# A state-space scan feeding a bilinear FFN on one core: constants made in another order on GpSimd, decay exponents kept in the PSUM banks of C·B, and a new instruction plan

## The chip, the core and the metric

The kernel runs on one core of a Trainium2 chip. A core has five engines that run their own instruction queues in order and wait for each other through semaphores: TensorE (PE, with its weight loads shown apart as PEld), VectorE (DVE), ScalarE (ACT), GpSimd (POOL) and SyncE (SP, which here issues the DMAs). Matmuls write into PSUM, eight banks of 512 fp32 columns by 128 partitions. The metric is the device time of one execution in microseconds.

## The reference, cut to what matters

Two stages follow each other. The first is a chunked scan over a sequence of 768 steps, for 4 batches and 8 heads, with a head size of 32 and a state of 16:

```python
for c in range(nc):
    cum = np.cumsum(la, axis=-1)                      # la = log(clip(a, 1e-6, 1)) of this chunk
    L = np.exp(cum[:, :, :, None] - cum[:, :, None, :]) * causal
    M = np.einsum('bhin,bhjn->bhij', Cc, Bc) * L
    y[:, :, sl] = M @ xc + (Cc @ state) * np.exp(cum)[..., None]
    state = np.exp(sum(la)) * state + sum_j decay_from_j * Bc (x) xc
```

The second is a feed-forward net over the 3072 tokens, with the scan's 256 features as input:

```python
h = (x @ w1) * (x @ w2) @ w3       # 256 -> 1024, 1024 -> 1024
out = h @ w_out                    # 1024 -> 256
```

The weights arrive as float64. The kernel multiplies w3 and w_out once on the chip, so that the net is one "up" step (two products and their product by elements) and one "down" step.

## The kernel before

**Tiling.** The sequence is cut into 16 chunks of 48 steps; two chunks make a slice of 96 steps, which with 4 batches gives 384 tokens. There are 8 slices. Per slice the net has 8 up steps `l<slice>.<ft>` (two halves `.0` and `.1` of six matmuls of 384 columns each) and 3 down steps `z<slice>.<tk>`. Numbers are kept as a sum of two reduced-precision parts, a high and a low one, which is why each product needs three matmuls.

**The order.** Everything is a named task, and the string `PLAN` lists the tasks; each engine executes its share of them in that order. Suffixes `:v`, `:a` and `:p` put a task on VectorE, ScalarE or GpSimd, and `+n` puts n matmuls on zeros there, which only keep TensorE occupied. The banks of the up and down steps come from a ring over banks 4, 5 and 6 (lines 189 to 197).

**A chunk `c<k>`.** `D0`, `D1` (line 392): TensorE forms the exponents (differences of cumulated logs) of 8 of the 16 head pairs each; for the first two chunks as an fp32 product with a triangular constant `LS` and a bf16 product with an identity `IM`, from chunk 2 on as one bf16 product of `LD` and `RD`. `E0`, `E1` (line 404): ScalarE takes their exponential into `rr`. `C` (line 422): 16 small products give C·B. `M0` to `M3` (line 411): VectorE multiplies C·B by the exponentials. `B0`, `B1` (line 407): GpSimd forms the decayed B. `Y` (line 435): 32 pairs of products give the output and the next state in one bank, called py. `Z` (VectorE) and `x0` to `x3` carry the state to the next chunk; `h` (ScalarE) and `l` (VectorE) write the high and low parts of the output, the input of the up steps. The function `at_of` (line 223) deals the banks 0 to 3 out in turn to the seven outputs of a chunk.

**Weights.** Each of 32 pieces of weights goes through six steps: `D` (DMA), `A` (scale, VectorE or ScalarE), `Y` (a copy of half words), `L` and `S` (bit operations, VectorE), `H` (high part) and `P` (low part). Names are `w0` to `w7` for w1 and w2 (`w0` and `w1` as two halves a and b), `o0` to `o3` for w_out and `v0` to `v15` for w3, whose products with w_out (`v<j>.M`) TensorE adds up in bank 7.

**The start.** `k.u` makes a triangular mask `UT`, `k.q` the constant `LS`, `k.p` makes `LD`, `k.c` makes `IM`, `k.r` a mask for the scan and `k.g` makes `RD`, all on GpSimd with memsets and selects (lines 271 to 317). `b.clip`, `b.ln` and `b.m<chunk><half>` prepare the first two chunks' logs, and `a.clip`, `a.ln`, `a.scan`, `a.t0`, `a.r0`, `a.t1`, `a.r1`, `a.save` the cumulated logs of all others, which go to memory and come back as rows of `LD` and `RD` (`c<k>.K`).

**The end.** `store_b` (line 638) writes a down step's 128 tokens; those of the last step lie in two batches, so there are two DMAs, of 32 and of 96 rows, both issued by SyncE.

Of the kernel before, what the change touches and what calls it, by code (L numbers as in the profile page):

```python
# [29 lines left out]
k.z b.D k.u b.tab k.p a.D w0b.D s0.N0 k.c w0a.D b.clip k.r c0.T b.ln b.m00:v w1a.D a.clip:p c0.X b.m01:v k.q  # L30
a.ln a.exp a.scan +8 c0.D1 c1.T k.X b.m10:v c1.X w0b.A:v w0b.Y:v s0.N1 +1 c0.D0 c0.E1 w0b.L a.t0:v k.L1:a c0.B1
b.m11:v c0.E0 w2.D a.r0:v c0.C w0a.A:v c0.B0 w0b.S c1.D1 k.g a.t1:v w0a.Y:v c0.S c0.M3 c0.M2 w0a.L a.r1:v c1.D0
c0.M0 c0.x0:a a.save w1a.A:v w1b.D c0.M1 c1.E1 w0a.S w3.D c1.C c1.E0 w0b.H:v w1a.Y:a c1.B1 c0.Y c1.B0 c1.M3
c0.x1:a c1.M2 k.R0:p c1.M1 w0a.H:a c1.M0 c2.X c0.h w1a.L k.R1:p +1 c1.Y c0.l s1.N w0b.P:v c2.K w0a.P:v c1.h
w1a.S c1.l +2 l0.0.1 w1b.A:a w2.A:v w1b.Y:a l0.0.0 w1a.H:v w1a.P:v w2.Y:a l0.0.0q w1b.L l0.0.1q w1b.S c2.T c1.Z
l0.1.0 l0.0.a w4.D c1.x2:p w2.L c1.x1:a c1.x3:a c1.x0:p w2.S w1b.H:a w5.D l0.1.a w1b.P:v w3.A:a +2 l0.1.1 l0.0.g
w2.H:v w3.Y:a c3.T c2.D1 w2.P:v c3.K c2.D0 l0.2.0 l0.1.g c2.E0 c2.E1 w3.L c2.B0 l0.2.1 w3.S c2.B1 l0.2.a w6.D
w3.H:v w4.A:a c2.C w3.P:v w4.Y:a l0.3.0 c2.M2 c2.M3 c2.M0 c2.M1 l0.3.1 c3.X w5.A:a w4.L w4.S l0.3.a c2.Y w5.Y:a
l0.2.g w4.H:p l0.3.g s2.N c2.Z w4.P:v c2.x0:p c2.h w7.D c3.D1 c3.D0 c2.x1:p c2.x2:a l0.4.1 c2.l c3.E0 o0.D w5.L
c3.E1 c4.K c3.B0 w6.A:a l0.4.0 w5.S c3.B1 c2.x3:a c4.T w5.H:v w6.Y:a c3.C w5.P:v c4.X l0.5.0 c3.M0 l0.4.a c3.M3  # L40
w6.L l0.5.1 w6.S l0.5.a c3.M2 o1.D w7.A:a w6.H:p c3.M1 l0.5.g c3.Y w7.Y:a w6.P:v l0.4.g l0.6.1 v0.D c3.Z o0.A:a
w7.L c3.x2:p l0.6.0 c3.h c5.K w7.S o0.Y:a c3.l w7.H:p l1.0.0 v1.D c3.x3:v l0.6.a c5.T w7.P:v c3.x0:a o3.D c4.D0
c3.x1:a c4.D1 o0.L l1.0.1 c4.E0 o0.S l1.0.a c4.B0 c4.E1 c5.X l1.1.1 l0.6.g o0.H:p o1.A:a l1.0.g c4.B1 o1.Y:a
o0.P:v c4.C l1.1.0 c4.M2 c4.M1 c4.M0 v0.A:v l0.7.0 v2.D l1.1.a o1.L v0.Y:a o2.D c4.M3 l0.7.1 l1.1.g o1.S v1.A:a
c4.Y v0.L o1.H:p v3.D v1.Y:a v0.S l1.2.0 o1.P:v v0.H:a v6.D v1.L l0.7.a c5.D1 l1.2.a c5.D0 v0.P:v l1.2.1 c5.E0
c4.Z c5.E1 c5.B0 v1.S c4.h l1.3.1 c4.x0:p o3.A:a c4.x1:p l1.2.g v7.D v1.H:p o3.Y:a v0.M c4.l c5.B1 l0.7.g
c4.x3:p v1.P:v v2.A:a o3.L l1.3.0 v2.Y:a o3.S c4.x2:v v1.M v5.D l1.3.a v2.L o2.A:a l1.3.g o3.H:a o2.Y:v l1.4.1
v2.S v3.A:a l1.4.0 o3.P:v v8.D v2.H:a o2.L v3.Y:a c5.C c6.X o2.S l1.5.0 c6.T c5.M0 l1.4.a c5.M3 v4.D c5.M2
o2.H:a l1.5.1 l1.4.g c6.K v6.A:a v3.L c5.M1 l1.5.a l1.6.0 v2.P:v v6.Y:a l1.5.g c5.Y o2.P:v l1.6.a v7.A:a v3.S
l1.7.0 v6.L v5.A:a v3.H:p v6.S l1.7.1 v5.Y:a v3.P:v v9.D l1.6.1 l1.7.a c5.Z v5.L v8.A:a c5.x2:p s3.N v5.S v2.M  # L50
v12.D c5.h c5.x1:a l1.6.g c5.x3:a c5.l v11.D c5.x0:a v3.M v8.Y:a l1.7.g v5.H:p v7.Y:v v5.P:v l2.0.0 e0.a v6.H:p
v4.A:v l2.1.0 e0.b v4.Y:a v6.P:v l2.0.1 l2.1.a v7.L l2.0.a v4.L v9.A:a v4.S l2.1.1 c7.K l2.0.g v9.Y:a l2.2.1
v8.L v10.D v8.S c7.T v4.H:a l2.2.0 v7.S v14.D v4.P:v v13.D c6.D1 l2.2.a c6.D0 v9.L v4.M c6.E0 v9.S c6.E1 c6.B0
v11.A:v v15.D c6.B1 v11.Y:a l2.1.g v5.M v7.H:p l2.2.g v12.A:v v7.P:v v12.Y:a v6.M c8.K v8.H:v v8.P:v c6.C
v10.A:v v9.H:a v11.L v7.M v10.Y:a c6.M2 c6.M1 v9.P:v v14.A:a c6.M0 c7.D1 l2.3.0 c6.M3 c8.T e1.a v11.S c7.E1 e1.b
c6.Y v14.Y:a c7.B1 v10.L v10.S v8.M v13.A:a c6.Z v10.H:p l2.3.a v14.L c6.h c6.x0:p v10.P:v v15.A:a v9.M v11.H:p
c7.X v15.Y:a c6.l c6.x3:p v11.P:v c6.x1:p c7.D0 l2.4.0 v13.Y:a v12.L v12.S v10.M c7.E0 v14.S l2.4.a c7.B0
v12.H:a v13.L v13.S c7.C v12.P:v v11.M v13.H:a c7.M1 c7.M0 v13.P:v c8.D0 e2.a v14.H:p l2.3.1 c7.M2 c7.M3 c8.E0
e2.b l2.4.1 l2.3.g v14.P:v l2.5.0 l2.4.g c6.x2:v v15.L l2.5.1 l2.5.a v15.S c8.D1 l2.5.g v12.M c8.E1 v13.M
v15.H:v v15.P:v s4.N v14.M v15.M c8.B0 l2.7.0 c8.B1 e3.a l0.0.h e3.b l2.6.1 l0.6.h l0.0.l:v l0.1.h l0.6.l:p  # L60
l0.5.h l2.6.0 l0.1.l:v l0.2.h l0.5.l:p l0.3.h l0.2.l:v c8.C l2.6.a l0.4.h l0.3.l:v c7.Y c9.K l2.7.a l2.6.g
l0.4.l:p l1.4.h c8.M1 l2.7.1 l1.0.h c7.Z l0.7.h l1.4.l:v l1.0.l:p l1.1.h l0.7.l:v z0.0 l1.6.h l1.1.l:p l1.5.h
c8.X l2.7.g l1.3.h l1.7.h c7.x0:v l1.6.l:p l1.2.h l1.3.l:v c10.K c7.h l1.7.l:p c7.x1:a z0.2 c8.M0 y0.0 c7.x2:v
y0.0b l1.2.l:p c7.l y0.0d c7.x3:v l1.5.l:p c9.T c8.M3 c8.M2 z0.1 y0.2 y0.2b y0.2d z1.0 y0.1 l2.4.h y0.1b c9.X
l2.7.h l2.4.l:p l2.2.h y0.1d l2.7.l:v l2.1.h l2.2.l:p l2.3.h l2.1.l:v l2.6.h z1.1 y1.0 l2.6.l:p l2.0.h y1.0b
l2.5.h l2.0.l:v y1.0d l2.3.l:p c10.T l2.5.l:p z1.2 y1.1 y1.1b y1.1d s5.N c9.D0 y1.2 c9.D1 l3.0.1:4 c9.E0 y1.2b
c9.E1 c9.B0 y1.2d c9.B1 l3.0.0:4 l3.1.0:4 l3.0.a l3.0.g l3.1.1:4 l3.1.a l3.0.h l3.2.0:4 l3.0.l:p l3.1.g l3.1.h
c9.C l3.2.a l3.1.l:p l3.2.1:4 c9.M1 c11.K c9.M0 c9.M2 c9.M3 c10.D0 c10.D1 l3.2.g l3.3.1:4 l3.2.h l3.2.l:v
# [33 lines left out]
def kernel(  # L102
# [279 lines left out]
    def chunk(c):  # L382
# [36 lines left out]
        for r in range(4):  # L419
            step(f"M{r}")(lambda e, r=r: weigh(r))  # L420
# [335 lines left out]
```

## Time and profile before

| what | value |
|---|---|
| median of 3 runs | 289.69 us (287.48, 289.74, 289.69) |
| the profiled execution | 286.1 us, of which the span between first and last instruction is 284.4 us |
| VectorE, ScalarE, GpSimd busy | 161.3 us, 149.8 us, 101.2 us |
| DMA | 29.30 MB, mean 103 GB/s |

The profiled execution is 1.2% below the median. Its span leaves 1.7 us outside. The share of busy time is an average: DMA, VectorE and ScalarE are nearly full in the first third, while weights are converted, and have much room in the rest.

### The profile page before, as it was taken

To read this page: it belongs to the slowest core of one execution; us is meant where nothing else is said; L and a number is where in the kernel's file an instruction comes from. 1 tells how busy PE (TensorE), PEld (TensorE's weight loads), DVE (VectorE), ACT (ScalarE), POOL (GpSimd) and SP (SyncE) were. 2 spreads that over 40 slices of the span, in tenths; PEclk is the share of its full clock that TensorE was granted. 3 is DMA by queue.
4 is the path that set the end of the run, shared out by engine and by line. 5 is a ranking of instruction groups with operands and counts; after the bars stand their busy time and mean duration, and the time that the engine had idled before them with its cause. 6 is when DMAs were issued, how large, how long until landed. Compare 5 with 4: busy or idle time off the path is not lost.

```text
span 284.4 us, 7390 instructions
## 1 busy us (share of the span) xinstructions
PE 273.7 (96%) x3010; PEld 242.8 (85%) x3010; DVE 161.3 (57%) x335; ACT 149.8 (53%) x288; POOL 101.2 (36%) x150
## 2 busy tenths in 40 slices
PE   4998999999999999999999999999999999999994
PEld 1477788999899998789998889989989998999884
DVE  4789999999999939862455244224351352122110
ACT  4189898999789319263352355315532443234211
POOL 8553422402125208672262125505440534044200
PEclk9799999999999999999999999999999999999999
DMA  5878968868492000145020240042211000100011
GB/s 168 217 210 285 287 184 291 292 204 284 137 336 75 28 5 2 40 118 154 8 76 7 64 133 6 2 121 63 61 30 39 22 1 2 37 18 2 18 53 39
DMA packets 22853, 29.30 MB, mean 103 GB/s; under 512 B 5540, under 2 KB 13220, under 8 KB 22820
## 3 DMA queue, kind: packets, MB, share of 16 engines
q1 hardware_dynamic: 22820, 28.84, 33.4%
q8 instruction: 23, 0.38, 0.6%
q14 instruction: 10, 0.08, 0.1%
HBM read 25.54 MB, written 3.29 MB: 101 GB/s over the span
## 4 chain that ended last, share of the span: by engine, by line
PE 76%; DVE 11%; issue 3%; ACT 3%; POOL 2%; DMA 2%; SPq 0%; DVEq 0%; POOLq 0%; ACTq 0%
PE bank L159 76%; DVE g L168 2%; DVE mag L527 2%; DVE gf L168 2%; DVE st L522 1%; DMA ld<-cd 1%; DVE rr L168 1%; DMA gf<-in_a_dram 1%; ACT st L165 1%; POOL ls L272 1%; DVE w L168 1%; ACT gf L165 1%; DVE wfl L168 1%; DVE zz L464 1%; ACT g L165 0%
## 5 line engine op out<-in xcount | busy, mean ns | idle before, releaser
L159 PE MATMUL bank<-xt,w 128*128 128x384 f32 x768 | 146.3, 342 | 0.9 <-DVE w L168 0.4
L159 PEld LDWEIGHTS bank<-xt,w 128*128 128x128 f32 x768 | 132.3, 188 | 6.0 <-ACT gf L165 1.4
L168 POOL TENSOR_TENSOR g<-gf,g 128x384 fp32r<-128x384 f32 x50 | 53.6, 1080 | 67.3 <-ACT g L165 67.2
L159 PE MATMUL bank<-wo,g 128*128 128x256 f32 (+1 forms) x392 | 69.2, 335 | 0.5 <-DVE gf L168 0.3
L159 PEld LDWEIGHTS bank<-wo,g 128*128 128x128 f32 x392 | 59.6, 188 | 9.2 <-DVE gf L168 0.9
L168 DVE TENSOR_TENSOR gf<-gf,bank 128x384 f32<-128x384 f32 x64 | 35.0, 551 | 51.0 <-PE bank L159 39.8
L165 ACT CAST g<-gf 128x384 fp32r<-128x384 f32 x64 | 31.0, 514 | 36.3 <-DVE gf L168 36.3
L165 ACT COPY gf<-bank 128x384 f32<-128x384 f32 x64 | 31.4, 494 | 17.4 <-PE bank L159 16.6
L165 ACT COPY st<-st 128x512 uint16<-128x512 uint16 (+1 forms) x26 | 34.6, 1341 | 1.5 <-DMA ld<-cd 0.7
L165 ACT COPY ob<-bank 128x256 f32<-128x256 f32 x24 | 8.9, 372 | 49.4 <-PE bank L159 46.9
L168 DVE TENSOR_TENSOR ob<-ob,bank 128x256 f32<-128x256 f32 x23 | 9.7, 420 | 44.4 <-ACT ob L165 42.0
L168 POOL TENSOR_TENSOR rr<-bn,rr 128x128 f32<-128x128 f32 x32 | 14.9, 476 | 52.5 <-ACT rr L405 47.6
L527 DVE SCALAR_TENSOR_TENSOR mag<-mag,st 128x512 uint32<-128x512 uint32 (+1 forms) x30 | 21.2, 712 | 0.7
L168 DVE TENSOR_TENSOR rr<-bank,rr 128x192 f32<-128x192 f32 x64 | 19.2, 346 | 3.1 <-PE bank L159 3.0
L159 PE MATMUL bank<-wfh,vh 128*128 128x256 f32 x64 | 18.8, 294 | 0.0
L159 PEld LDWEIGHTS bank<-rr,xe 64*32 64x32 f32 x1024 | 15.3, 107 | 3.9 <-issue 2.8
L405 ACT ACTIVATE rr<-bank 128x384 f32<-128x384 f32 x32 | 14.8, 496 | 7.1 <-PE bank L159 6.2
L165 POOL COPY xe<-zz 16x256 f32<-16x256 f32 x24 | 11.7, 488 | 17.8 <-DVE zz L464 16.8
L159 PE MATMUL bank<-rr,xe 64*32 64x64 f32 x1024 | 17.9, 218 | 0.1
L159 PE MATMUL bank<-wfl,vh 128*128 128x256 f32 x64 | 17.9, 279 | 0.0
L159 PE MATMUL bank<-wfh,vl 128*128 128x256 f32 x64 | 17.9, 279 | 0.0
L509 ACT ACTIVATE mag<-st 128x512 f32<-128x512 f32 (+1 forms) x21 | 14.4, 692 | 0.0
(71 smaller groups left out, 218.4 us busy)
## 6 DMA issues: line engine op xcount, KB each, us to landing
st<-in_w3t_dram SPq DMA_DIRECT2D x16, 512.0 KB
st<-in_w_dram SPq DMA_DIRECT2D x16, 256.0 KB
xe<-in_x_dram SPq DMA_DIRECT2D x32, 96.0 KB
bc<-in_Bt_dram SPq DMA_DIRECT2D x8, 320.0 KB
bc<-in_Ct_dram SPq DMA_DIRECT2D x8, 320.0 KB
st<-in_w_out_dram SPq DMA_DIRECT2D x4, 512.0 KB
bn<-in_Bn_dram SPq DMA_DIRECT2D x7, 256.0 KB
out_dram<-ob SPq DMA_DIRECT2D x16, 96.0 KB
```

Of the source, the lines that this page charges most:

```text
L159: return tc.keep_in_program_order(nc.tensor.matmul(*args, **kw))
L165: return ins(nc.scalar.copy(*args) if eng == "a" else {"v": nc.vector, "p": nc.gpsimd}[eng].tensor_copy(*args))
L168: return ins({"v": nc.vector, "p": nc.gpsimd}[eng].tensor_tensor(*args))
L272: ins(nc.gpsimd.affine_select(out=t, in_=t, pattern=pattern, compare_op=op, fill=value, base=base, channel_multiplier=step))
L405: ins(nc.scalar.activation(R[:, hf * G8:(hf + 1) * G8, N:], v["pd", hf], AF.Exp))
L464: ins(nc.vector.transpose(ZZ.rearrange("p k b d -> p (k b) d"), v["py"].rearrange("p k b m -> p (k b) m")[:, :, 0:32]))
L509: ins(nc.scalar.activation(v["mag"], v["wh"], AF.Copy, scale=2.0 ** -112))
L522: ins(nc.vector.tensor_scalar(w, w, 13, 7 - 2 ** 31, ALU.arith_shift_right, ALU.bitwise_and))
L527: ins(nc.vector.scalar_tensor_tensor(mi, mi, 3, v["wh"].bitcast(U32), ALU.logical_shift_left, ALU.bitwise_or))
```

## The change

**Constants.** `k.q` goes ahead of `k.p`, `k.c` and `k.r` on GpSimd. `a.clip` goes from GpSimd to VectorE, the copies `k.L1` and `a.t0` go to GpSimd.

**Banks.** Banks 0 to 5 become three tiles of two banks, `PAIR[0]` to `PAIR[2]`. From chunk 2 on C·B takes columns 0 to 191 of banks 0 to 3 and the exponents take columns 192 to 383 of the same banks, `D0` in banks 0 and 1, `D1` in banks 2 and 3. Each `D` is therefore two matmuls of 192 columns in place of one of 384. `E0` and `E1` read a pair of banks in one instruction. `M0` to `M3`, of one bank each, become `M0` and `M1`, of a pair each. `at_of` is gone: py is in bank 0 until chunk 6, and in bank 7 after that, so that `D0` of the chunk after and py share a bank.

**The plan.** `ORDER` and `PLAN` are new throughout. The `+n` add up to 21 in place of 14. They stand at other places, and write into the bank of `c0.S` or bank 6.

**The last store.** Its piece of 32 rows is issued by ScalarE, the other one still by SyncE.

```diff
 PLAN = """
-k.z b.D k.u b.tab k.p a.D w0b.D s0.N0 k.c w0a.D b.clip k.r c0.T b.ln b.m00:v w1a.D a.clip:p c0.X b.m01:v k.q
+k.z b.D k.u b.tab k.q s0.N0 a.D s0.N1 k.p w0b.D b.clip c1.X b.ln b.m00:v k.c w0a.D b.m01:v k.r +7 c0.D0 c0.X k.X
...
-    bank = [ps.tile([P, 512], F32, name=f"bank{i}") for i in range(8)]
+    PAIR = [ps.tile([P, 2, 512], F32, name=f"bank{i}") for i in range(3)]
+    bank = [PAIR[i // 2][:, i % 2] for i in range(6)] + [ps.tile([P, 512], F32, name=f"bank{i}") for i in (6, 7)]
...
-    def at_of(c, k):
-        if c < CPS:
-            return bank[((0, 1, 2, 3, 4, 5, 1), (6, 0, 2, 3, 4, 5, 0))[c][k]]
-        return bank[(7 * c + k) % 4 if c < CPS * (NLAG + 1) - 1 else (0, 1, 0, 1, 2, 3, 7)[k]]
+    def py_of(c):
+        return bank[(1, 0)[c] if c < CPS else 0 if c < CPS * (NLAG + 1) - 1 else 7]
...
             if sl:
-                mm(pd, ld, RD[:, c % 2, gs].rearrange("p g s -> p (g s)"), start=True, stop=True)
+                w = G8 // 2 * T
+                v["pd", hf] = PAIR[hf][:, :, w:2 * w].rearrange("p k (g s) -> p k g s", s=T)
+                for k in range(2):
+                    g0 = hf * G8 + k * G8 // 2
+                    mm(PAIR[hf][:, k, w:2 * w], ld, RD[:, c % 2, g0:g0 + G8 // 2].rearrange("p g s -> p (g s)"),
+                       start=True, stop=True)
...
-        def weigh(r):
-            gs = slice(r * NG // 4, (r + 1) * NG // 4)
-            tt("v", R[:, gs, N:], v["pc", r], R[:, gs, N:], ALU.mult)
+        def weigh(hf):
+            t = R[:, hf * G8:(hf + 1) * G8, N:].rearrange("p (k g) s -> p k g s", k=2)
+            pc = PAIR[hf if sl else hf + 1][:, :, :G8 // 2 * T].rearrange("p k (g s) -> p k g s", s=T)
+            tt("v", t, pc, t, ALU.mult)
...
-            load(out[r0:r0 + n, :], ob[t0 - tk * P:t0 - tk * P + n, :])
+            load(out[r0:r0 + n, :], ob[t0 - tk * P:t0 - tk * P + n, :], eng="a" if (sl, tk) == LAST and n < SL else None)
```

The lists that follow are the instructions of one engine in its order. A name ends in a tile's number; in the changed kernel `bank0_77`, `bank1_78` and `bank2_79` are the three pairs, so that `bank1_78` is banks 2 and 3.

GpSimd before, from the first constant on (`ls` is the constant of the first exponents, `ld` and `im` those of their second half, line 337 the clip of `a`):

```order
L272 AFFINE_SELECT ut_95<-ut_95 64x48
L292 MEMSET ld_92 102x128
L272 AFFINE_SELECT ld_92<-ld_92 102x64 x6
L300 MEMSET im_97 48x48
L272 AFFINE_SELECT im_97<-im_97 48x48
L305 MEMSET gf_67 128x192
L306 MEMSET gf_67 128x4
L337 TENSOR_SCALAR gf_67<-gf_67 128x192
L283 MEMSET ls_96 112x128
L272 AFFINE_SELECT ls_96<-ls_96 112x64 x4
```

GpSimd in the changed kernel, at the same place:

```order
L269 AFFINE_SELECT ut_92<-ut_92 64x48
L280 MEMSET ls_93 112x128
L269 AFFINE_SELECT ls_93<-ls_93 112x64 x4
L289 MEMSET ld_89 102x128
L269 AFFINE_SELECT ld_89<-ld_89 102x64 x6
L297 MEMSET im_94 48x48
L269 AFFINE_SELECT im_94<-im_94 48x48
L302 MEMSET gf_67 128x192
L303 MEMSET gf_67 128x4
L314 MEMSET xe_69 16x512 x2
L163 COPY ld_89<-ld_89 102x128
L163 CAST gf_67<-gf_67 128x192
```

The clip is gone, and `ls` is made first; the identity `im` comes after it.

ScalarE before, around chunk 3 (`xt` is `c2.h`; lines 405 are `c3.E0` and `c3.E1`; `st` copies are `Y` steps of weights; `gf` copies are `l0.<ft>.a`):

```order
L165 CAST xt_68<-bank0_77 128x8x48
L165 COPY xe_69<-zz_73 16x8x32
L405 ACTIVATE rr_70<-bank1_78 128x8x48
L405 ACTIVATE rr_70<-bank2_79 128x8x48
L509 ACTIVATE mag_89<-st_88 128x512
```

ScalarE in the changed kernel, at the same place:

```order
L163 CAST xt_68<-bank0_77 128x8x48
L410 ACTIVATE rr_70<-bank1_78 128x8x48
L163 COPY xe_69<-zz_73 16x8x32 x2
L163 COPY st_85<-st_85 128x512
L163 COPY gf_67<-bank6_80 128x384
L410 ACTIVATE rr_70<-bank0_77 128x8x48
L514 ACTIVATE mag_86<-st_85 128x512
```

The two exponentials of the chunk stood next to each other; now `c3.E1` comes first, and a `Y` step and a copy of an up step stand ahead of `c3.E0`.

More of the change, by code (lines that the diff above doesn't have):

```diff
@@ L35 @@
[L35 to L44, printed above, removed]
@@ L418, in chunk @@
             step(f"B{hf}")(lambda e, hf=hf: bw(hf))
-        for r in range(4):
-            step(f"M{r}")(lambda e, r=r: weigh(r))
+            step(f"M{hf}")(lambda e, hf=hf: weigh(hf))
         @step("C")
@@ L677, in keep_clock @@
         for _ in range(n):
-            mm(bank[7 if "c0.S" in tasks else 6], zero[:, 0:P], zero, start=True, stop=True)
+            mm(bank[6 if "c0.S" in done else 7], zero[:, 0:P], zero, start=True, stop=True)
+    done = set()
     for name in PLAN.split():
@@ L685 @@
             tasks.pop(name)(e or None)
+            done.add(name)
     assert not tasks, list(tasks)
```

131 lines of the change are left out of this document (70 added, 61 removed), and 2 rows, old and new, of the table ORDER.

## The prediction

> **What bounds the kernel now.** I read the page first, then the busy time by stretches, then who waits for whom, and last the instructions of the start.
>
> ```profile
> PE 273.7 (96%) x3010; PEld 242.8 (85%) x3010; DVE 161.3 (57%) x335; ACT 149.8 (53%) x288; POOL 101.2 (36%) x150
> PE   4998999999999999999999999999999999999994
> PEclk9799999999999999999999999999999999999999
> ```
>
> TensorE is busy in every slice but the first and the last. So only time in which it has nothing to do, or a slow clock, or too much to do, can change the total. The stretches say where that is (busy time and count by engine, clock, DMA share, GB/s):
>
> ```profile
> 7.49:11.10 3.61, 3.61 (x6) 1.12 (x6) 2.91 (x8) 0.68 (x2) 1.40 (x3) 0.53 1.04 274
> 11.10:19.35 8.25, 8.05 (x268) 4.99 (x267) 6.45 (x18) 4.60 (x10) 5.76 (x8) 1.00 0.60 178
> 19.35:25.65 6.30, 5.08 (x29) 4.49 (x29) 5.79 (x15) 6.06 (x10) 1.15 (x2) 1.00 0.81 248
> 25.65:39.35 13.70, 13.24 (x245) 10.96 (x243) 13.12 (x28) 12.17 (x20) 5.11 (x8) 1.00 0.92 276
> 39.35:75.00 35.65, 35.28 (x390) 32.40 (x384) 34.46 (x69) 33.04 (x53) 9.71 (x16) 1.00 0.75 245
> 75.00:106.00 31.00, 31.00 (x337) 29.37 (x338) 26.05 (x52) 18.92 (x29) 7.91 (x13) 1.00 0.36 114
> 106.00:116.00 10.00, 9.48 (x137) 7.83 (x136) 9.37 (x12) 9.12 (x22) 8.31 (x8) 1.00 0.01 2
> 116.00:280.66 164.66, 164.65 (x1606) 150.65 (x1604) 59.88 (x129) 61.30 (x141) 55.80 (x70) 1.00 0.17 47
> 6.13:20.19 14.06, 12.50 (x277) 6.95 (x278) 11.49 (x32) 7.08 (x15) 8.51 (x14) 0.88 0.77 219
> ```
>
> From 116 us to the end of its work TensorE never rests: 164.65 of 164.66 us. Nothing in that stretch can be won, only lost. Between 19.35 us, where the first up step starts, and 116 us it idles 1.22 + 0.46 + 0.37 + 0.52 = 2.57 us. What is left is the start: 19.35 us go by before the first up step. Between 20 and 75 us VectorE and ScalarE are themselves nearly full, so there TensorE and the conversion of weights run neck and neck.
>
> The waits of TensorE, and one of ScalarE that I use later (total, times, longest):
>
> ```profile
> PE bank L159 <- POOL ls L272: 2.8, 1, 2.8
> PE bank L159 <- ACT gf L165: 1.6, 2, 1.2
> ...
> ACT xt L165 <- DVE zz L464: 3.1, 6, 0.8
> ```
>
> The largest one is for GpSimd's constant `ls`. The start by instructions (start, duration):
>
> ```profile
> 1.29 3.35 PE L159 MATMUL bank<-zero 128*128 128x512 bf16 x8 [1.29 <-DVE zero L266]
> 1.76 1.22 POOL L272 TENSOR_SCALAR_AFFINE_SELECT ld<-ld 102x64 bf16<-102x64 bf16 x6
> 3.12 0.22 POOL L272 TENSOR_SCALAR_AFFINE_SELECT im<-im 48x48 bf16<-48x48 bf16 x1
> 3.49 1.03 DVE L168 TENSOR_TENSOR gf<-a,ut 112x384 f32<-112x384 f32 x2 [0.36 <-ACT a L329]
> 4.03 1.19 POOL L337 TENSOR_SCALAR gf<-gf 128x192 f32<-128x192 f32 x1 [0.33 <-DMA gf<-in_a_dram]
> 5.56 1.88 POOL L272 TENSOR_SCALAR_AFFINE_SELECT ls<-ls 112x64 f32<-112x64 f32 x4
> 5.65 0.56 DVE L339 TENSOR_TENSOR_SCAN gf<-gf 128x192 f32<-128x192 f32 x1 [1.14 <-ACT gf L338]
> 7.49 1.51 PE L159 MATMUL bank<-gf,ls 112*128 112x384 f32 x2 [2.85 <-POOL ls L272]
> ...
> 19.64 0.55 DVE L168 TENSOR_TENSOR xt<-bank,xt 128x384 fp32r<-128x384 f32 x1
> ...
> 24.82 0.69 DVE L168 TENSOR_TENSOR w<-mag,w 128x512 fp32r<-128x512 f32 x1
> ```
>
> TensorE's zeros end at 4.64, it idles to 7.49, and then works at a clock of 0.53 until 11.10.
>
> **The change part by part.** The durations of one instruction (busy, mean ns), by shapes:
>
> ```profile
> L168 DVE TENSOR_TENSOR gf<-gf,bank 128x384 f32<-128x384 f32 x64 | 35.0, 551 | 51.0 <-PE bank L159 39.8 <-ACT gf L165 10.9
> L165 ACT COPY st<-st 128x512 uint16<-128x512 uint16 x24 | 33.1, 1389 | 1.4 <-DMA ld<-cd 0.7 <-DVE mag L512 0.2
> L165 ACT COPY gf<-bank 128x384 f32<-128x384 f32 x64 | 31.4, 494 | 17.4 <-PE bank L159 16.6 <-DVE gf L168 0.6
> L168 DVE TENSOR_TENSOR rr<-bank,rr 128x192 f32<-128x192 f32 x64 | 19.2, 346 | 3.1 <-PE bank L159 3.0
> L405 ACT ACTIVATE rr<-bank 128x384 f32<-128x384 f32 x32 | 14.8, 496 | 7.1 <-PE bank L159 6.2 <-POOL g L168 0.8
> L159 PEld LDWEIGHTS <-ld 102*128 102x128 bf16 x28 | 1.9, 99 | 2.3 <-issue 1.9 <-DMA st<-in_w3t_dram 0.2
> L165 ACT COPY xe<-bank 16x512 f32<-16x512 f32 x2 | 1.2, 576 | 2.3 <-PE bank L159 2.3
> L165 DVE CAST gf<-gf 128x192 bf16<-128x192 f32 x2 | 0.9, 450 | 0.0
> L165 DVE CAST w<-mag 128x256 fp32r<-128x256 f32 x2 | 0.8, 393 | 0.0
> ```
>
> *The start.* On GpSimd `ls` now follows `ut`, whose selects are done before 1.76; 0.2 for the memset and 1.88 for four selects put it at 3.7. The first log products on VectorE are ready at about 4.0 (half of 1.03 after 3.49). TensorE's first exponents can start near 4.1 in place of 7.49. Their second half needs `im`, which is now behind `ls` and `ld`: 3.7 + 1.22 + 0.22 and two memsets, about 5.5. So TensorE gains some 3.4 us, and with its zeros running up to 4.2 it has no idle stretch like that from 4.64 to 7.49.
>
> That is not what reaches the end, because the first up steps wait for VectorE: `c1.l` (19.64 to 20.19) and the low parts of the first weights. I count VectorE's queue from the end of the scan to `c1.l`. Before, it is 11.49 us of work in 14.06 us. The change takes out `a.t0` (0.45) and `w0b.H` (0.39), puts in `c0.x0` (0.58, as on ScalarE), and makes four of 0.551 out of eight of 0.346 (less 0.56): 11.49 - 0.45 - 0.39 + 0.58 - 0.56 = 10.67. The scan itself moves little: the load of `a` is issued one place later (some 0.4 us), the clip leaves GpSimd's 1.19 us for VectorE (I take 0.4), and a scaling of weights now stands ahead of the scan; I put its end at 6.4, against 5.65 + 0.56 = 6.21. With no waits `c1.l` would be done at 6.4 + 10.67 = 17.1, a gain of 3.1. With all the 2.57 us of waits of that stretch it would be 19.6, a gain of 0.6. Most of those waits were for TensorE's late exponents and C·B, which now come earlier, so I take 0.7 us of waits: done at 17.8, gain **2.4**.
>
> *The conversion stage, 20 to 40 us.* The lead holds only where VectorE and ScalarE keep it. For `w2.P`, which ended at 24.82 + 0.69 and released the third up step, VectorE has about the same work as before, so it comes some 2 us earlier; the plan has seven of the zeros just ahead of that step, in the wait (0.21 each at full clock, half of 3.35/8, so 1.5 us if that wait were not there). At chunk 3 the order on ScalarE is worse: a `Y` step of 1.389 and a copy of 0.494 stand ahead of `c3.E0`, `c3.M0` waits for that, and `c3.Y` on TensorE for `c3.M0`, with only the exponents of chunk 4 between. That can cost between nothing and 1.88 us of lead. Against it stand the 1.22 + 0.46 us of idle time that the stretch had before. I take 2.0 us of idle time in place of 1.68: **-0.3**, between -1.9 and +1.7.
>
> *From 40 to 116 us* there were 0.37 + 0.52 us of idle time. `M0` and `M1` save 2 x 346 - 551 = 141 ns twice per chunk on VectorE, some 2 us in nine chunks, but TensorE hardly waited for it there. I take **0**, between 0 and +0.9.
>
> *Exponents as two matmuls.* 14 chunks have two each, so 28 more matmuls and 28 more weight loads, all of them on TensorE's path. The columns stay the same. The upper bound is that every extra weight load of 99 ns stands open: 28 x 99 = 2.8 us. The lower one is nothing, since weight loads run beside matmuls. I take 18 ns each, near the lower end, because in the last long stretch 150.65 us of weight loads lie beside matmuls without a gap in TensorE's work: **-0.5**. ScalarE's exponentials read the same elements as before, from two banks in place of one; I cost that at nothing, since ScalarE has room after 75 us.
>
> *The last store.*
>
> ```profile
> 275.92 5.95 SPq L162 DMA_DIRECT2D out_dram<-ob  x6
> ...
> 280.68 0.37 ACT L165 COPY ob<-bank 128x256 f32<-128x256 f32 x1 [2.45 <-PE bank L159]
> ```
>
> After the last copy ends at 281.05 SyncE issues two stores one behind the other, until 281.87: 0.41 each. With the first one on ScalarE the second goes out 0.41 earlier: **+0.4**, between 0 (if ScalarE's issue is as late as the second was) and 0.41.
>
> Sum: 2.4 - 0.3 + 0 - 0.5 + 0.4 = 2.0 us. The profiled execution's 286.1 would become 284.1. The median of the runs is 3.6 us above that execution, and I add this: 289.7 - 2.0 = 287.7 us. A measurement of this kernel tells 1%, some 2.9 us, from no change, so this lies within it.
>
> **The rivals.**
>
> *All waits close (faster).* VectorE has less to do in every stage, and if the new plan fits its queues, the start brings 3.1 and all of the 2.57 us of later idle time goes: 3.1 + 2.6 - 0.5 + 0.4 = 5.6 us, 284.1 us. For it speaks the lighter VectorE; against it the order on ScalarE at chunk 3, and that ScalarE is as full as VectorE from 25 to 75 us.
>
> *The lead is lost again.* If `c3.E0` costs the whole 1.88 us and nothing else improves, 2.4 - 1.9 - 0.5 + 0.4 = 0.4 us are left: 289.3 us. A second way to the same place is the clock: if TensorE still got a stretch at 0.53, as from 7.49 to 11.10, its work up to the first C·B would take about 1.7 us longer, and VectorE would wait for it; the gain at the start falls to about 0.7. The trace shows that stretch behind an idle time of 2.85 us, and the new order has none as long, by my count 0.7 at most. The Trainium skill ("TensorE: Matmul & The Clock Gate", section "What's actually happening") says that the clock is halved after an idle window of about 3.4 us whose phase is free-running; the rows here agree with half a clock after an idle stretch of about that size, and by that rule too the changed kernel would stay at full clock.
>
> *Shared banks make a chain (slower).* Exponents and C·B now lie in the same four banks. The wait of `xt` for `zz` above shows that two readers of one bank, ScalarE and VectorE, take turns in this kernel. If TensorE may not write C·B while ScalarE reads exponents of the same bank, each of the 14 chunks can hold TensorE for one exponential, 0.496: 6.9 us, and 287.7 + 6.9 = 294.6 us. It decides from 0.35 us per chunk on (14 x 0.35 = 4.9, which takes the 2.0 back and 2.9 more). Against it: the plan puts up steps between `D1` and `C` of a chunk, and after 116 us there is other work for TensorE all the time. The Trainium skill ("PSUM — Partial Sum Buffer", section "PSUM bank collisions raise a hardware error") says that two engines on the same bank and the same 32 partitions must be kept apart, also at different columns; that is a rule against this change, and by it the time would be this rival's 294.6 us unless other work covers the waits. The one row here, a reader behind a reader, agrees with it.
>
> **How the numbers follow.** I give the forecast (a gain of 0.4 to 3.2 us) 0.50, the closing of all waits 0.30, the lost lead 0.13, the chain over the banks 0.07. The predicted time is that of the first, 287.7 us. The range reaches to the two middle rivals and a little past them, from 284.0 to 290.2 us; the chain is left out, and the ends of the others. Faster by over 1% is the second case and the upper edge of the first, 0.36; slower by over 1% is the chain, 0.07; within 1% is the rest, 0.57.
>
> **What would show each step.** The start: the first `gf,ls` matmul near 4.1 us, no row with a clock near 0.5 after 7.5 us, and the first up step near 17 us; at 19 it is wrong. The conversion stage: a wait of TensorE for `rr` at `c3.Y` of about 1 us, behind `c3.E0`. The two-part exponents: TensorE's time from the end of the conversions to its last matmul longer by 0.3 us or so; 1.5 us would mean that weight loads stand open. The banks: waits of TensorE for ScalarE's `rr` ahead of `C`, small and few; if they add up to more than 2 us, the chain is real. The end: 3.3 us from the last matmul to the end in place of 3.7. The forecast as a whole is wrong if TensorE's idle time between its first up step and 116 us is below 1 us or above 4.

## The result and the profile after

The changed kernel takes 316.05 us (median of 4 runs, 314.1 to 316.21); the kernel before took 289.01 us on the same chip (4 runs, 287.48 to 289.74). The ratio is 1.093, with a 95% interval of 1.086 to 1.099: the change makes the kernel 9.3% slower, where a gain of 0.7% had been forecast. The profiled execution has 314.1 us and a span of 312.4. The medians and ratios further down leave out three runs that were slow as a whole, one of front_alone (288.31 us) and two of own45_c3 (290.44 and 290.46).

The page of the changed kernel, busy time, slices and chain:

```profile
PE 282.8 (91%) x3045; PEld 245.5 (79%) x3045; DVE 156.6 (50%) x300; ACT 148.0 (47%) x284; POOL 101.2 (32%) x157
...
PE   8888799898999987989997999999999999999993
...
PE 63%; DVE 13%; ACT 11%; DMA 6%; issue 3%; POOL 1%; SPq 1%; DVEq 0%; ACTq 0%; POOLq 0%
```

The start is better (8 in place of 4 in the first slice), but TensorE no longer stays at 9: the loss is spread over the whole span. The waits of TensorE (total, times, longest) say for whom:

```profile
PE bank L157 <- ACT gf L163: 9.4, 16, 1.2
PE bank L157 <- DVE rr L166: 4.2, 2, 2.9
PE bank L157 <- DVE gf L166: 3.4, 5, 0.9
PE bank L157 <- DVE ob L166: 1.6, 2, 0.9
```

The readers of up and down steps (`gf`, `ob`) hold TensorE up. The stretches (busy time and count of TensorE first, granted clock, DMA share and GB/s last) put this late, where TensorE had never rested before:

```profile
18.68:25.65 6.97, 6.97 (x66) 5.39 (x67) 5.46 (x14) 6.81 (x11) 1.87 (x4) 1.00 0.78 223
...
120.00:309.00 189.00, 174.20 (x1722) 154.46 (x1720) 60.52 (x116) 65.17 (x149) 57.23 (x74) 0.99 0.14 39
sum 290.32, PE 268.01 PEld 238.37 DVE 145.04 ACT 140.43 POOL 87.67; mean PE 44.67 PEld 39.73 DVE 24.17 ACT 23.40 POOL 14.61
```

The chain of work in slice 7 (start, duration, what) shows how:

```profile
272.94 2.39 PE bank L157 x12
275.35 0.49 ACT gf L163
...
275.87 0.57 DVE gf L166
...
276.48 2.38 PE bank L157 x12
...
280.10 0.39 ACT gf L163
...
280.53 2.39 PE bank L157 x12
```

TensorE writes the twelve matmuls of banks 4 and 5, ScalarE copies out, VectorE multiplies, and only then the next twelve start; in between there is only the six of bank 6 to do. TensorE's share of the chain falls from 76% to 63%.

From the first up step (18.68) to the last matmul (the final copies begin at 307.28) it is 288.6 us, against 261.3 before: +27.3. The start is 0.7 shorter, the end 1.4 longer (5.1 in place of 3.7): together 28.0, the difference of the spans. Of the 288.6 us TensorE idles 288.6 - 268.0 = 20.6, against 2.6 before. The other 9 us are in the busy time that the page counts. They are not the work of the 33 matmuls that the change adds here: after_own45, below, runs the same 2763 matmuls of this stretch in 257.1 us of busy time. The longer end is the same wait from the reader's side. The last two copies on ScalarE:

```profile
307.28 0.37 ACT L163 COPY ob<-bank 128x256 f32<-128x256 f32 x1 [5.25 <-PE bank L157]
...
308.14 0.37 ACT L163 COPY ob<-bank 128x256 f32<-128x256 f32 x1 [0.49 <-DVE ob L166]
```

The first of them, of the down step before the last one, waits 5.25 us until the matmuls of the last one are done as well.

### The profile page after: what moved, and what is told of

The parts are those of the page before. It is cut to its first block, busy times and chain, and to the rows that moved or that the text cites. A ratio compares the mean times of both kernels' runs of the same rounds, so it can differ in the third digit from the quotient of the medians.

```text
span 312.4 us, 7439 instructions
## 1 busy us (share of the span) xinstructions
PE 282.8 (91%) x3045; PEld 245.5 (79%) x3045; DVE 156.6 (50%) x300; ACT 148.0 (47%) x284; POOL 101.2 (32%) x157
## 4 chain that ended last, share of the span: by engine, by line
PE 63%; DVE 13%; ACT 11%; DMA 6%; issue 3%; POOL 1%; SPq 1%; DVEq 0%; ACTq 0%; POOLq 0%
PE bank L157 63%; DVE gf L166 4%; ACT gf L163 4%; ACT st L163 2%; ACT g L163 2%; DMA st<-in_w3t_dram 2%; DMA xe<-in_x_dram 2%; DVE rr L166 1%; DMA st<-in_w_out_dram 1%; DVE mag L532 1%; POOL rr L166 1%; DMA st<-in_w_dram 1%; DVE g L166 1%; DVE st L527 1%; ACT rr L410 1%
## 5 line engine op out<-in xcount | busy, mean ns | idle before, releaser
L157 PE MATMUL bank<-xt,w 128*128 128x384 f32 x768 | 148.6, 343 | 13.9 <-ACT gf L163 8.8
L166 POOL TENSOR_TENSOR g<-gf,g 128x384 fp32r<-128x384 f32 x49 | 51.3, 1052 | 118.4 <-ACT g L163 118.2
L157 PE MATMUL bank<-wo,g 128*128 128x256 f32 (+1 forms) x392 | 70.9, 341 | 3.0 <-DVE gf L166 1.4
L157 PEld LDWEIGHTS bank<-wo,g 128*128 128x128 f32 x392 | 60.8, 192 | 12.3 <-DVE gf L166 2.1
L163 ACT COPY st<-st 128x512 uint16<-128x512 uint16 (+1 forms) x24 | 32.2, 1364 | 1.6 <-DVE mag L517 1.2
L166 POOL TENSOR_TENSOR rr<-bn,rr 128x128 f32<-128x128 f32 x32 | 15.6, 504 | 17.3 <-ACT rr L410 16.8
L532 DVE SCALAR_TENSOR_TENSOR mag<-mag,st 128x512 uint32<-128x512 uint32 (+1 forms) x30 | 20.6, 694 | 0.5
L166 DVE TENSOR_TENSOR rr<-bank,rr 128x384 f32<-128x384 f32 x32 | 17.0, 549 | 4.6 <-PE bank L157 2.0
L163 POOL COPY xe<-zz 16x256 f32<-16x256 f32 x29 | 13.1, 451 | 12.8 <-DVE zz L469 11.8
L514 ACT ACTIVATE mag<-st 128x512 f32<-128x512 f32 (+1 forms) x23 | 15.9, 691 | 0.5 <-issue 0.5
```

The costliest lines, as they stand in the source:

```text
L157: return tc.keep_in_program_order(nc.tensor.matmul(*args, **kw))
L163: return ins(nc.scalar.copy(*args) if eng == "a" else {"v": nc.vector, "p": nc.gpsimd}[eng].tensor_copy(*args))
L166: return ins({"v": nc.vector, "p": nc.gpsimd}[eng].tensor_tensor(*args))
L514: ins(nc.scalar.activation(v["mag"], v["wh"], AF.Copy, scale=2.0 ** -112))
L532: ins(nc.vector.scalar_tensor_tensor(mi, mi, 3, v["wh"].bitcast(U32), ALU.logical_shift_left, ALU.bitwise_or))
```

## The experiments

All times in us; "before" stands for the kernel before on the same chip in the same session: 288.32 (17 runs) beside the first four rows, 288.57 (23) beside the second four, 288.33 (21) beside the last four. The three sessions ran on three chips. A kernel that ran once has no ratio. The other ratios are estimated from all the runs counted, and so differ a little from the quotients of the medians.

| run | median (runs) | ratio to before |
|---|---|---|
| before_pair45 | 311.19 (3) | 1.079 [1.073, 1.085] |
| after_own45 | 285.74 (12) | 0.993 [0.989, 0.996] |
| split_decays | 289.02 (1) | |
| last_store | 288.06 (1) | |
| own45_py0 | 284.51 (6) | 0.985 [0.981, 0.990] |
| own45_c3 | 287.84 (10) | 0.996 [0.992, 1.000] |
| own45_both | 286.91 (12) | 0.993 [0.990, 0.996] |
| front_alone | 283.97 (5) | 0.984 [0.979, 0.990] |
| before_z18 | 284.56 (6) | 0.987 [0.984, 0.990] |
| front_z4 | 286.44 (8) | 0.991 [0.988, 0.995] |
| own45_c3m0 | 285.97 (10) | 0.991 [0.988, 0.994] |
| own45_zeros | 285.46 (10) | 0.990 [0.987, 0.993] |

### Two banks in one tile

**before_pair45**, the kernel before with this alone:

```diff
-    bank = [ps.tile([P, 512], F32, name=f"bank{i}") for i in range(8)]
+    two = ps.tile([P, 2, 512], F32, name="two")
+    bank = [two[:, i - 4] if i in (4, 5) else ps.tile([P, 512], F32, name=f"bank{i}") for i in range(8)]
```

> The kernel before, with one edit: banks 4 and 5 are two halves of one tile, in place of two tiles. No instruction changes, and neither does the order. Theory 1 (waits are set per tile of PSUM, so the ring of three banks for the up and down steps becomes a ring of two): a matmul into bank 4 then also waits for the readers of bank 5, TensorE stands still for ScalarE's and VectorE's copies of `gf` after each pair of up steps, and from 116 us on the time grows; 308 to 318 us, with some 12 us or more of TensorE waits for `gf`. Theory 2 (the exponents that share banks with C·B make the chain) and theory 3 (the new plan is bad): nothing happens, 287 to 290 us.

**after_own45**, the changed kernel with banks 4 to 7 as tiles of their own (the product `M1` of the first two chunks, which read banks 4 and 5 in one instruction, becomes two instructions for that):

```diff
-    PAIR = [ps.tile([P, 2, 512], F32, name=f"bank{i}") for i in range(3)]
-    bank = [PAIR[i // 2][:, i % 2] for i in range(6)] + [ps.tile([P, 512], F32, name=f"bank{i}") for i in (6, 7)]
+    PAIR = [ps.tile([P, 2, 512], F32, name=f"pair{i}") for i in range(2)]
+    bank = [PAIR[i // 2][:, i % 2] for i in range(4)] + [ps.tile([P, 512], F32, name=f"bank{i}") for i in range(4, 8)]
```

> The changed kernel with banks 4 and 5 as tiles of their own again; in exchange the second C·B product of chunks 0 and 1, which lies there, is two instructions of one bank each on VectorE. Theory 1: TensorE's waits for `gf` fall from 12.8 us to below 2, and the time comes back to 284 to 290 us; what then still differs from the kernel before is what my prediction was about. Theory 2: TensorE still waits at the C·B of each chunk, 305 us or more. Theory 3: 305 us or more, with waits spread over the first 116 us.

The first puts most of the loss into the old kernel: no instruction is new, their order is the same, and it takes 22.9 us more. TensorE's waits in it, by the name of the new tile:

```profile
PE two L159 <- ACT gf L165: 5.2, 10, 0.8
...
PE two L159 <- DVE gf L168: 2.2, 5, 0.7
PE two L159 <- DVE ob L168: 2.2, 3, 0.9
```

With 2.1 us more in a row of the single banks, the waits for `gf` come to 9.5 us, less than the 12 expected. Between the first up step and its last matmul TensorE idles 15.9 us, against 2.6 before, and the same 2730 matmuls are busy for 266.0 us, against 258.7; as in the changed kernel, a part of the loss lies inside the busy time.

The second takes the loss out of the changed kernel: 30.3 us less than the changed kernel as it is. (Why the pairing costs more under the new plan than under the old was not tried.) Its waits for readers of banks 4 to 6 are nearly gone:

```profile
PE pair L157 <- DVE rr L166: 2.7, 2, 1.6
...
PE bank L157 <- ACT xt L163: 1.1, 1, 1.1
...
PE bank L157 <- DVE gf L166: 0.5, 1, 0.5
PE bank L157 <- ACT gf L163: 0.5, 2, 0.3
```

So the program's waits are set for a tile of PSUM and not for a bank (two edits in opposite directions, of the tiles alone but for `M1`, show it). With banks 4 and 5 in one tile, a matmul into bank 4 also waits for whoever reads bank 5, and the ring of three banks turns into one of two places. The banks themselves can be written and read next to each other: the same matmuls run without these waits as soon as the tiles are apart. All else that the change does is a gain of 2.6 us by the medians.

### The small terms

**split_decays**, the kernel before with each bf16 exponent product cut in two:

```diff
-                mm(pd, ld, RD[:, c % 2, gs].rearrange("p g s -> p (g s)"), start=True, stop=True)
+                for g0 in range(hf * G8, (hf + 1) * G8, G8 // 2):
+                    o = (g0 - hf * G8) * T
+                    mm(pd[:, o:o + G8 // 2 * T], ld, RD[:, c % 2, g0:g0 + G8 // 2].rearrange("p g s -> p (g s)"),
+                       start=True, stop=True)
```

> The kernel before, with each of the 28 bf16 products of exponents cut into two matmuls of 192 columns, in the same bank. My prediction took 0.5 us for it, with 0 and 2.8 as bounds. From 116 us to TensorE's last matmul there are 14 of the 28 products: 0.25 us more there by my value, 1.4 us if each extra weight load of 99 ns stands open, nothing if the loads hide. Theories 1 to 3 of the slowdown are not touched by this: all three expect 287 to 290 us.

**last_store**, the kernel before with the 32-row store on ScalarE:

```diff
-            load(out[r0:r0 + n, :], ob[t0 - tk * P:t0 - tk * P + n, :])
+            load(out[r0:r0 + n, :], ob[t0 - tk * P:t0 - tk * P + n, :], eng="a" if (sl, tk) == LAST and n < SL else None)
```

> The kernel before, with the last 32-row store issued by ScalarE. My prediction: the second store goes out 0.4 us earlier, and from the last copy's start (280.68 us before) to the end of the span there are 3.3 us in place of 3.7. If ScalarE's issue is later than SyncE's second one was, nothing changes. The time itself cannot show 0.4 us in one run.

There is one run of each, so they are read by stretches. The first up step and the last copy, whose start marks the end of the last matmul, of split_decays (span 287.4):

```profile
22.19 1.14 PE L159 MATMUL bank<-xt,w 128*128 128x384 f32 x5
...
283.63 0.37 ACT L165 COPY ob<-bank 128x256 f32<-128x256 f32 x1 [2.45 <-PE bank L159]
```

From one to the other it is 261.44 us, against 261.33 (19.35 to 280.68) before: 28 more matmuls and weight loads cost 0.1 us. The same rows and the new store of last_store (span 286.4):

```profile
21.58 1.68 PE L159 MATMUL bank<-xt,w 128*128 128x384 f32 x8
...
282.90 0.37 ACT L165 COPY ob<-bank 128x256 f32<-128x256 f32 x1 [2.45 <-PE bank L159]
283.30 0.39 ACTq L162 DMA_DIRECT2D out_dram<-ob  x1
```

From that copy to the end of the span it is 3.5 us, against 3.72 before and 3.77 in split_decays: the second queue saves 0.2 to 0.3.

### The start and the clock

split_decays has the start of the kernel before to the letter, and yet its first up step comes at 22.19, not at 19.35. The three experiments here ask why, and what an early `ls` is worth by itself.

**front_alone**, the kernel before with the constant `ls` built early:

```diff
-k.z b.D k.u b.tab k.p a.D w0b.D s0.N0 k.c w0a.D b.clip k.r c0.T b.ln b.m00:v w1a.D a.clip:p c0.X b.m01:v k.q
+k.z b.D k.u b.tab k.q k.p a.D w0b.D s0.N0 k.c w0a.D b.clip k.r c0.T b.ln b.m00:v w1a.D a.clip:p c0.X b.m01:v
```

> The kernel before with GpSimd's building of ls right behind ut and nothing else (no pairs, old plan). Prediction's start term: the first gf,ls near 4.2 us instead of 7.49, the first up step up to 2.4 us earlier, time 287.3 us or less. Theory now: the work between (zeros, im,ld, the Y matmuls, GpSimd's other constants, which now come later) and the clock of TensorE, which is not at full speed before about 11 to 15 us whatever the work, take most of it: the first up step 0 to 1 us earlier, time within 1 us of before (288.3).

**before_z18** (`+8 c0.D1` becomes `+18 c0.D1` in the kernel before) and **front_z4** (`+8` becomes `+4` in front_alone):

> The kernel before with 18 instead of 8 matmuls of zeros ahead of the first gf,ls, which still waits for ls until 7.5 us; nothing else. Theory, the idle 2.85 us of TensorE ahead of the first gf,ls cost the full clock, and that is the larger part of what an early ls brings: the zeros fill the gap, the first gf,ls (7.5 to 7.9 us) takes 0.9 us instead of 1.5 to 1.65, the first up step comes at 18.0 to 18.8 us instead of 19.35 to 22.2, and the time is 285 to 287 us with less spread (288.5 before). Rival, it is the wait for ls itself that costs: the first up step at 19.4 or later and no change of the time, or 1 us more if the added zeros run cold past 7.5 us.

> front_alone (ls built early, 283.99 us) with 4 instead of 8 matmuls of zeros ahead of the first gf,ls: TensorE idles some 2 us ahead of it. Theory of the clock: the first gf,ls stay near 5.2 us but take 1.5 us and more each, the first up step comes at 18.5 to 20.5 us instead of 17.51, time 285.5 to 288 us. Rival, the early ls alone makes the gain: first up step and time as front_alone (284.0).

The first matmuls of TensorE (start, duration, count, idle time ahead), first front_alone:

```profile
1.29 3.60 PE L159 MATMUL bank<-zero 128*128 128x512 bf16 x8 [1.29 <-DVE zero L266]
5.22 0.88 PE L159 MATMUL bank<-gf,ls 112*128 112x384 f32 x2 [0.33 <-DVE gf L168]
...
17.51 3.40 PE L159 MATMUL bank<-xt,w 128*128 128x384 f32 x18
```

before_z18:

```profile
1.29 5.53 PE L159 MATMUL bank<-zero 128*128 128x512 bf16 x18 [1.29 <-DVE zero L266]
7.18 0.91 PE L159 MATMUL bank<-gf,ls 112*128 112x384 f32 x2 [0.36 <-POOL ls L272]
...
17.56 3.40 PE L159 MATMUL bank<-xt,w 128*128 128x384 f32 x18
```

front_z4:

```profile
1.29 1.89 PE L159 MATMUL bank<-zero 128*128 128x512 bf16 x4 [1.29 <-DVE zero L266]
5.41 1.62 PE L159 MATMUL bank<-gf,ls 112*128 112x384 f32 x2 [2.23 <-DVE gf L168]
...
19.95 3.39 PE L159 MATMUL bank<-xt,w 128*128 128x384 f32 x18
```

Ten matmuls on zeros do what the early constant does. In before_z18 the first exponents still wait for `ls` (they start at 7.18, against 7.49 before) and yet the first up step comes at 17.56, sooner than the 18.0 to 18.8 expected, because the idle 2.85 us ahead of the first exponents are filled and a pair of exponent products takes 0.91 us in place of 1.51. front_z4 has the early `ls` but idles 2.23 us, its first exponents take 1.62 us, and by the medians 1.9 us are left of the 4.6 us of front_alone (six of its runs lie from 286.4 to 287.5, two at 283.8 and 283.9). The runs of before_z18 lie closer together, too: 284.42 to 285.52, against 287.3 to 289.79 of the kernel before beside it. What was taken for a wait for a constant was for the most part a slow TensorE behind that wait. The expectation for front_alone (within 1 us of before) was wrong; the prediction's term was nearer.

The profiles taken together say the same. From the first up step to the start of the last copy on ScalarE it takes 261.33 us in before, 261.44 in split_decays, 261.32 in last_store, 261.00 in front_alone, 261.22 in before_z18 and 261.41 in front_z4, while the first up step itself lies anywhere from 17.51 to 22.19. What sets these executions apart is almost the start alone.

### Where the changed kernel loses its lead again

In the changed kernel py of chunk 0 is in bank 1 and py of chunk 1 in bank 0, two halves of one tile. **own45_py0** is after_own45 with py of chunk 0 in bank 6:

```diff
-        return bank[(1, 0)[c] if c < CPS else 0 if c < CPS * (NLAG + 1) - 1 else 7]
+        return bank[(6, 0)[c] if c < CPS else 0 if c < CPS * (NLAG + 1) - 1 else 7]
```

> The changed kernel with banks 4 to 7 as tiles of their own (after_own45), and py of chunk 0 in bank 6 instead of bank 1, so that it shares no tile with py of chunk 1 (bank 0). Theory, waits are set per tile: in after_own45 ScalarE's first cast of xt (c0.h) starts at 19.66 us, right after the matmuls of c1.Y end (19.62), though those of c0.Y end at 17.6. Alone in its tile it starts near 17.7, the two casts of w behind it too, the cast of chunk 1 right after c1.Y, and the first up step (21.30 us there) comes up to 1.1 us earlier against the end of c1.Y: within 0.7 us behind it instead of 1.7. Time 0.5 to 1.1 us below after_own45, near 284.9 us. Rival, the first up step waits for w0's words on VectorE or ScalarE: c0.h moves and the first up step does not, time as after_own45 (285.7).

ScalarE's first cast of `xt` and the first up step of after_own45, where the last matmul of `c1.Y` ended at 19.62:

```profile
19.66 0.48 ACT L163 CAST xt<-pair 128x384 fp32r<-128x384 f32 x1 [2.92 <-PE pair L157]
...
21.30 3.03 PE L157 MATMUL bank<-xt,w 128*128 128x384 f32 x15 [1.14 <-ACT xt L163]
```

and of own45_py0, where it ended at 17.91:

```profile
16.41 0.48 ACT L163 CAST xt<-bank 128x384 fp32r<-128x384 f32 x1 [0.57 <-PE bank L157]
...
18.49 4.69 PE L157 MATMUL bank<-xt,w 128*128 128x384 f32 x24 [0.26 <-ACT xt L163]
```

The cast no longer waits for the other chunk, and the first up step follows `c1.Y` by 0.58 us in place of 1.68: 1.1 us won, and the medians, of two sessions, differ by 1.2. (The first up step comes 2.8 us earlier in all; the rest of that is ahead of `c1.Y`, where after_own45 happened to run its exponents slowly up to 13 us and this execution only up to 6 us.) Again two banks in one tile hold a reader up, here for a writer of the neighbour.

**own45_c3** and **own45_both** move `c3.E0` ahead of the `Y` step that stood before it, in after_own45 and in own45_py0:

```diff
-c4.T w5.Y:a c3.D0 c3.C o0.D l0.4.1 c3.M1 l0.4.a w5.L c3.E0 w6.A:a
+c4.T c3.D0 c3.C o0.D l0.4.1 c3.M1 l0.4.a c3.E0 w5.Y:a w5.L w6.A:a
```

> after_own45 with c3.E0 ahead of w5.Y on ScalarE (w5.Y and w5.L right behind c3.E0). Theory of rival 2 of the prediction, c3.Y waits because E0 of chunk 3 stands behind the 1.36 us of Y and a copy: the wait for rr ahead of c3.Y (1.62 us in after_own45) falls to 0.3 us or none, and the time falls by up to 1.3 us, unless the up step 0.5, whose words come 1.4 us later, takes the wait over: then no change in time (within 0.5 us) and a wait for w, or for mag, ahead of l0.5.0.

> Both edits of own45_py0 and own45_c3 together. If the two waits are independent their gains add: 0.5 to 1.1 us and 0 to 1.3 us below after_own45, 283.4 to 285.2 us; if the conversions of w set the time until 40 us, the first one's gain is lost again ahead of an up step of 0.1 to 0.5, and the time is that of after_own45 (285.7).

**own45_c3m0** is own45_py0 with `w5.Y:a` behind `c3.E0` and `w5.L w5.S` behind `c3.M0`, and **own45_zeros** is that with `+8` in place of the `+7` ahead of the first exponents.

> own45_py0 (284.51 us) with w5.Y behind c3.E0 on ScalarE as in own45_c3, and on VectorE c3.M0 ahead of the words of w5 (L and S of w5 behind it), since in own45_c3 and own45_both the product M0 stood behind them. Theory, c3.Y waits for that product alone: the wait for rr ahead of c3.Y falls from 1.63 us (own45_py0) to 0.4 us or less, time 283.1 to 284.2 us, if the up step 0.5 does not wait for w5. Rival, words of w bound this stretch: the wait moves to l0.5.0 and the time is 284.5.

> own45_c3m0 with 8 instead of 7 matmuls of zeros ahead of the first gf,ls (7 end at 4.5 us and leave 0.3 us idle there). Theory of the clock: the first gf,ls take 0.9 us instead of 1.6, and the first up step comes 0.3 to 1.5 us earlier, with less spread of the runs; time 282.5 to 284 us, the fastest of all. Rival, the gap of 0.3 us does not matter: as own45_c3m0, or up to 0.3 us more.

`c3.Y` in after_own45, own45_both and own45_c3m0:

```profile
39.09 1.10 PE L157 MATMUL pair<-rr,xe 64*32 64x64 f32 x64 [1.62 <-DVE rr L166]
```

```profile
38.19 1.10 PE L157 MATMUL pair<-rr,xe 64*32 64x64 f32 x64 [2.24 <-DVE rr L166]
```

```profile
37.47 1.10 PE L157 MATMUL pair<-rr,xe 64*32 64x64 f32 x64 [0.26 <-DVE rr L166]
```

VectorE in own45_both, and a wait of TensorE that is new in own45_c3m0:

```profile
36.51 0.43 DVE L531 TENSOR_SCALAR st<-st 128x512 int32<-128x512 int32 x1 [1.23 <-ACT st L163]
...
37.59 0.55 DVE L166 TENSOR_TENSOR rr<-pair,rr 128x384 f32<-128x384 f32 x1
```

```profile
PE bank L157 <- DVE w L163: 0.9, 1, 0.9
```

With `E0` first the wait grew, since VectorE now stood at the words of `w5` (1.23 us idle) ahead of `c3.M0`: the edit had moved the obstacle from one queue to the other. At 286.91 own45_both is slower than both outcomes expected for it, and 2.4 us above own45_py0 of the same session; 0.7 of that is behind the first up step (261.45 us to the last copy, against 260.72). With `M0` ahead too the wait closes, a wait for `w` of 0.9 us opens, and the time does not fall (285.97 against 284.51 for own45_py0, of two sessions, runs that overlap). The same stretch shows it without the start: 260.72 us in own45_py0, 260.76 in after_own45, 261.06 in own45_c3m0 and 261.10 in own45_zeros. So closing this wait wins nothing; the wait for `w` that opens in its place is what the rival expected of the conversion of weights. The first up step of own45_c3m0 comes at 21.02, against 18.49 in own45_py0, though the edit lies behind it; that lateness, and not chunk 3, is why its profiled execution is the longer one. (In it TensorE stands 2.09 us at 15.53 for VectorE's `rr`.) Why own45_c3, in another session, came out 2.1 us above after_own45 is open. The eighth matmul of zeros in own45_zeros brings the first exponents to full speed in its profile (0.88 in place of 1.62) and the first up step to 18.22, but its runs spread as much as without it (284.15 to 287.63, median 285.46, where 282.5 to 284 had been expected); why is open.

The fastest versions are front_alone, before_z18 and own45_py0, 1.3 to 1.6% below the kernel before and not to be told apart by these runs. The first two are also the simplest: each is the kernel before with one entry of its plan changed.

## Why the prediction was wrong

**The step that failed** is the pricing of the pairs. The prediction asked what shared banks do in "the same four banks", 0 to 3, for the rival of the chain, and said of the exponentials that read two banks "I cost that at nothing". The third pair, banks 4 and 5, was in the text of the change and got no term, though two thirds of the matmuls of the up steps go through it (516 of 768 write the new tile in before_pair45). The row that would have priced it was quoted: "From 116 us TensorE never rests", with three places in the ring. Six matmuls take 1.2 us; a copy of 0.49 and a product of 0.55 follow them. With three places two more groups can run beside those readers, with the pair only the group of bank 6. The runs: +22.9 us from this alone (before_pair45), and 30.3 us less when it is undone in the changed kernel (after_own45).

**The start, +2.4.** front_alone's first up step is 1.84 us earlier than in the profiled execution of before and 4.1 to 4.7 earlier than in split_decays (22.19) and last_store (21.58); its median is 4.6 us lower. The term was real. In the changed kernel it came to 0.7 (18.68): 1.1 us went to the py tiles, which couple the first two chunks (own45_py0), and no run divides up the rest. "The first `gf,ls` near 4.1 us" came at 4.26; "the first up step near 17 us, at 19 it is wrong" is closer to wrong.

**The median.** The prediction took the 3.6 us between the profiled execution and the median as a constant and added them. Most of them belong to the term at the start: the first up step of that execution came 2.2 and 2.8 us earlier than those of last_store and split_decays, which have the same start, since TensorE was fast sooner (from the exponents at 12.08 us on, 0.91 a pair; those at 12.65 in split_decays still took 1.65). With 17 to 23 runs the median is 288.3 to 288.6, only 2.2 to 2.5 us above that execution. A change that touches the start changes that difference.

**The clock as a rival.** The prediction gave it no more idle time than 0.7 us and so no slow stretch. It asked only what an idle stretch does; but TensorE is slow from its first matmul on: the eight zeros of front_alone take 3.60 us, and ten more only 1.93 (18 in 5.53 us in before_z18). In the changed kernel seven of them stand there with no idle time behind, and the first pair is slow and the second fast; in after_own45 they stand there with 0.35 us of idle time, and the slow stretch went on to 13 us:

```profile
4.26 1.59 PE L157 MATMUL bank<-gf,ls 112*128 112x384 f32 x2
...
6.86 0.81 PE L157 MATMUL bank<-gf,ls 112*128 112x384 f32 x2
```

```profile
1.30 3.17 PE L157 MATMUL bank<-zero 128*128 128x512 bf16 x7 [1.30 <-DVE zero L263]
4.81 1.62 PE L157 MATMUL pair<-gf,ls 112*128 112x384 f32 x2 [0.35 <-POOL im L269]
```

The Trainium skill ("TensorE: Matmul & The Clock Gate", section "What's actually happening") has the clock full after about 3.4 us of sustained work and halved by an idle window of that size, the windows being free-running: front_alone, at 0.88 after 3.60 us of zeros, agrees, and so do after_own45, at 1.62 after 3.17 us, and front_z4, at 1.62 after 1.89 us. In split_decays a pair at 1.65 stands behind 3.60 us of zeros and an idle time of only 2.63 us, which is less than such a window; whether the clock had been full before it, no row shows.

**The conversion stage, -0.3, and chunk 3.** The wait ahead of `c3.Y` was predicted at about 1 us and was 1.30 in the changed kernel and 1.62 in after_own45; closing it won nothing.

**Exponents in two, -0.5:** 0.1 in one run. **The last store, +0.4:** 0.2 to 0.3.

**The chain over banks 0 to 3, 294.6 us:** not there. after_own45 has all of it and is faster than before; TensorE waits for `rr` twice, 2.7 us in all and 1.6 of them ahead of `c3.Y`, where 14 waits and 6.9 us were the rival's price. The prediction's own argument against it, that the plan keeps other work in between, fits; it was not tried by itself.

After the coupling of banks 4 and 5 is taken out, the sum was about right: -2.0 forecast, 285.74 against 288.32 measured, -2.6 by the medians. In part that is luck, since the terms do not come out one by one. The profiled execution of after_own45 (287.2 us, above its median) has its first up step at 21.30, later than the 19.35 of before, so no trace shows the gain of the start in that kernel; and behind the start, where the sum had a loss of 0.8 us, it is 0.6 us shorter (260.76 against 261.33 to the last copy).

## What to carry to other kernels

Before banks are put together into one tile, list who writes and who reads each of them: if the waits are set per tile, a ring of buffers loses a place with each pair, and the price is the reader's time at every turn. At a start, look at how long the first matmuls take and not only at what they wait for; a few matmuls on zeros in the gap may be worth as much as a rearranged plan. A wait removed from one in-order queue has to be followed into the next one before it is counted.

## What the runs showed of the hardware

TensorE can stay slow for a long time while it works. In front_z4 it has hardly any idle time from 5.41 us on, and a pair of exponent products took 1.47 to 1.65 us each time until that at 14.34, against 0.81 to 0.91 in front_alone; by the rule cited above one full window of 3.4 us should have been enough, at the latest 6.8 us after the start of the work (an estimate from that figure of the Trainium skill's page). The granted clock of its rows does not show it:

```profile
7.50:12.00 4.50, 4.50 (x38) 1.79 (x37) 4.43 (x16) 1.57 (x5) 2.07 (x4) 1.00 1.05 286
```

This is front_z4, with a clock of 1.00 in a stretch where the products run at half speed; in the kernel before the same kind of stretch was shown at 0.53. So the durations of equal matmuls are to be read, and the clock column only beside them.

VectorE's times stretch beside GpSimd's selects: in own45_c3m0 a copy of 128x256 half words took 1.18 us while a pair of selects ran from 10.94 to 13.05, and 0.44 two microseconds earlier. In front_alone and before_z18 a scaling of 128x256 took 0.75 us beside the same selects and 0.28 ahead of them.

```profile
9.00 0.44 DVE L163 COPY st<-st 128x256 uint16<-128x256 uint16 x1
...
11.10 1.18 DVE L163 COPY st<-st 128x256 uint16<-128x256 uint16 x1
```

```profile
10.94 2.11 POOL L269 TENSOR_SCALAR_AFFINE_SELECT rd<-rd 102x768 bf16<-102x768 bf16 x2
```

In own45_py0 one such copy took 0.43; it had begun at 10.47, 0.01 us ahead of the selects, so it does not hit every time.
